# Rounded q and k: stored once per part, and stacked by two loads instead of one

## The chip, the cores and the metric

The kernel runs on one core of one Trainium2 chip. The metric is the device time of one launch in microseconds (us); the kernel before takes 719.64 us (median of 3 runs, 719.59 to 719.88).

The engines are named as in the profile: PE is TensorE (matrix multiplication), PEld its weight loads, DVE is VectorE, ACT is ScalarE, POOL is GpSimd, and SP is the engine whose queue issues nearly all DMAs of this kernel. DMA transfers are done by 16 DMA engines that these queues feed.

## The reference

The reference is one transformer block on 2048 tokens of width 448: layer norm, causal attention with 16 heads of 28 columns in a sliding window of 256 tokens, a residual sum, a second layer norm, a gated feed-forward part of width 1792, and a second residual sum. Cut to what matters:

```python
def _A_ref(x, wqkv, wo):
    H = 16; Dh = D // H; W = 256
    q, k, v = ...                      # x @ wqkv, split by heads
    scores = jnp.einsum("bhqd,bhkd->bhqk", q, k) * (Dh ** -0.5)
    mask = (idx[:, None] - idx[None, :] >= 0) & (idx[:, None] - idx[None, :] < W)
    scores = jnp.where(mask[None, None], scores, -1e9)
    p = _softmax(scores, axis=-1)
    o = jnp.einsum("bhqk,bhkd->bhqd", p, v)
    return o... @ wo

def _B_ref(x, w_gate, w_up, w_down):
    h = _gelu(x @ w_gate) * (x @ w_up)
    return h @ w_down

h = x + _A_ref(_layernorm(x), wqkv, wo)
out = h + _B_ref(_layernorm(h), w_gate, w_up, w_down)
```

All inputs and outputs are float32.

## The kernel before, in words

**Two parts for one number.** The matmuls run in a rounded 32-bit type (`F32R`). To keep float32 precision, a number is split into a rounded high part and the rest, the low part, and a product is made of three: high by high, high by low, low by high. For the scores, the three products are made in a single matmul: the 28 columns of a head are stacked three times along the partitions (84 rows). The stack of q holds high, low, high and the stack of k holds high, high, low, so the sum over the 84 rows is the sum of the three products.

**Projection.** The tokens are cut in 4 chunks (`CS`) of 512. `project_tile(c, m)` makes one of seven output tiles of a chunk with 11 matmuls (line 630): tile m is q or k of one of the groups of 4 heads (112 rows), and 16 further rows that belong to k of the last group. ACT rounds the result from PSUM to the high part, and DVE subtracts to get the low part. The two parts lie in a staging buffer taken by `pk_at`.

**Store.** `put` writes them to a DRAM tile of 112 rows, three rows of 512 per channel (`qk_d`). One DMA (line 640) reads the high part once and writes it to two of the three rows; a second one (line 642) writes the low part. The same pair is issued for the 16 further rows. Each tile thus issues four DMAs.

**Load.** `loads(B)` fetches block B, that is, 4 heads for 512 queries. B counts from 0 to 15, and the group is B % 4, the chunk B // 4. `get` fetches 256 tokens of q or k with one DMA (line 662): 84 partitions (28 channels by three rows) by 4 heads by 256 tokens. q goes to `rq[u]`, k to `rk[u]`, with u = B % 2, so two blocks have buffers. A block loads two halves of 256 tokens, each with one DMA for q and one for k, and from chunk 1 on a further load of the 256 tokens of k from the chunk before.

**Scores and the rest.** `scores` multiplies 128 queries by up to 384 keys of a head (line 680), and DVE takes the maximum over the masked result (line 684). `maxima` turns the maxima into rows that ACT puts beside the q stack (lines 711 and 353). `probs` multiplies again with keys as rows (line 755), now with 104 partitions: the 84 of the stack, zeros, and the rows for the maxima; ACT takes the exponential (line 759). POOL masks the edges (line 774), `attend` multiplies with v (line 793), `drain` normalises, and `output` multiplies with wo (line 851). The second layer norm and the feed-forward part follow (line 1000 and lines after it).

**What sets the order.** Nothing is issued when it is written down. Every step is recorded by `op` with an engine, a cost, a latency, a key and the names that it reads and writes (tokens such as `("rq", u, i)`). `Lists.run` then plays the whole program with these costs: on each engine it takes, among the steps that could start within a short time, the one with the lowest key, and issues it. So the order on every engine comes from the costs, the keys and the dependencies. For a DMA, the planner counts its size, a shared bus, a margin for arrival and at most eight transfers in flight:

```python
if e == "sp" and len(dmas) >= 8:
    t = max(t, dmas[-8])
...
bus = max(bus, t + 1.2) + o.size * 0.0034 + (1.25 if len(dmas) == 2 else 0)
```

Each engine then runs its list in order, and waits on semaphores. The eight DMA semaphores are used in turn, so the ninth DMA waits until the first has landed.

Of the kernel before, what the change touches and what calls it, by code (L numbers as in the profile page):

```python
# [8 lines left out]
F32 = mybir.dt.float32  # L9
# [6 lines left out]
S, D, H, DH, W, F = 2048, 448, 16, 28, 256, 1792  # L16
# [3 lines left out]
GF = 4 * DH  # L20
EPS = 1e-5
SCALE = float(DH) ** -0.5
CS = NT // 4
# [48 lines left out]
def mm(n):  # L72
    return max(n / 2400 + 0.0155, 0.115)
# [156 lines left out]
def block_kernel(ctx: ExitStack, tc, x, wqk_in, wv_in, wo_in, ffn_in, out):  # L230
    nc = tc.nc
# [7 lines left out]
    dram = ctx.enter_context(tc.tile_pool(name="dram", bufs=1, space=bass.MemoryType.DRAM))  # L239

    def f(ap):
        return ap.bitcast(F32)
# [25 lines left out]
    mhl = [mhl_m[:, 128 * i:128 * i + 128] for i in range(2)]  # L268
    rcp = [pool.tile([128, 16], F32, name=f"rcp{i}") for i in range(2)]

    qk_d = [[[dram.tile([GF, 3, 512], F32, name=f"{'qk'[i]}{g}_{c}") for i in range(2)] for c in range(CS)]
            for g in range(NG)]
    ffn_d = dram.tile([128, 1472], F32, name="ffn2")
    xn_d = [dram.tile([D, 128], F32, name=f"xn{t}") for t in range(NT)]
# [20 lines left out]
    rq = [rq_m[:, 2048 * u:2048 * u + 2048].rearrange("p (j t) -> p j t", j=4) for u in range(2)]  # L295
    rk = [rk_m[:, 3072 * u:3072 * u + 3072].rearrange("p (j t) -> p j t", j=4) for u in range(2)]
# [17 lines left out]
    def span(name, lo, n):  # L314
        return (name, lo, lo + n)
# [14 lines left out]
    def WQK(m, h):  # L330
        return ("wqk", m, h)
# [20 lines left out]
    def to_hi(dst, src):  # L352
        nc.scalar.activation(dst, src, AF.Copy)  # L353
# [4 lines left out]
    def dma(key, size, fn, r=(), w=(), cost=0.44, after=()):  # L358
        return op("sp", cost, 0, key, fn, r, w, size=size, after=after)
# [259 lines left out]
    def project_tile(c, m):  # L619
        g, s = divmod(m, 2)  # L620
        cc = 12 * (c % 2)
        hl, both, tok = pk_at()
        B = 4 * c + g
        b = Bank("proj")
        per = 1 if m == 6 else 2
        base = 16 * B - EDGE - (ELAST if c == 3 else 0)
        for a in range(NP):
            h, wb, xb = TERMS[a]
            key = -33 + 6 * m + a / 4 if B < 2 else base - WIN * (1 - (s * NP + a) / (per * NP))
            op("pe", mm(512) + 0.002, 0.403, key, lambda a=a, h=h, wb=wb, xb=xb: nc.tensor.matmul(  # L630
                bank[b.k], wqk[m][:, h, wb, :], xT[:, xb, cc * 128:cc * 128 + 512], start=(a == 0),
                stop=(a == NP - 1)), [span("xT", cc, 4), WQK(m, h)], (), b, tag="proj")
        key = -30 + 6 * m if B < 2 else base
        op("act", 0.49, 0.605, key, lambda: to_hi(hl[0], bank[b.k]), (), [tok[0]], b)
        op("dve", 0.603, 0.698, key, lambda: to_lo(hl[1], bank[b.k], hl[0]), [tok[0]], [tok[1]], b)


        def put(rows, d, name, s, size):
            n = rows.stop - rows.start
            dma(key, 458 * size, lambda: nc.sync.dma_start(  # L640
                d[:, 0:3 - s:2 - s], both[rows, 0:1].to_broadcast([n, 2, 512])), tok[0:1], [(name, 0)])
            dma(key, 229 * size, lambda: nc.sync.dma_start(d[:, 1 + s], both[rows, 1]), tok[1:2], [(name, 1)])
        put(slice(0, GF), qk_d[g][c][s], ("d", g, s, c), s, 1)
        put(slice(GF, 128), qk_d[NG - 1][c][1][16 * m:16 * m + 16], ("d", NG - 1, 1, c, m), 1, 0.15)


    def block(B):
        return B % 4, B // 4
# [3 lines left out]
    def loads(B):  # L652
        g, c = block(B)
        u = B % 2

        def get(s, cc, lo, n, at, key):
            src = qk_d[g][cc][s].rearrange("(j p) b t -> (p b) j t", j=4)[:, :, lo * 128:(lo + n) * 128]
            dst, tok = (rk, "rk") if s else (rq, "rq")
            rd = [(("d", g, 1, cc, m), i) for m in range(WT) for i in range(2)] if s and g == NG - 1 else \
                [(("d", g, s, cc), i) for i in range(2)]  # L660
            rd += [("zk" if s else "zq", u, i) for i in range(2)]
            dma(key, 246 * n, lambda: nc.sync.dma_start(f(dst[u][0:3 * DH, :, at * 128:(at + n) * 128]), src),
                rd, [(tok, u, at + i) for i in range(n)])
        key = 16 * B - (8 if B > 1 else 24)
        if c:
            get(1, c - 1, 2, 2, 0, key)
        for i in range(0, 4, 2):
            get(0, c, i, 2, i, key + 4 * i)
            get(1, c, i, 2, 2 + i, key + 4 * i)
        got[B] = L.ops[-1]  # L670

    def scores(B, i, j):
        g, c = block(B)
        u, m0 = B % 2, i if c else max(i, 2)
        b = Bank("score")
        o = (m0 - i) * 128
        s = 16 * B + 4 * i + j

        def one():
            nc.tensor.matmul(bank[b.k][:, o:384], rq[u][0:3 * DH, j, i * 128:i * 128 + 128],  # L680
                             rk[u][0:3 * DH, j, m0 * 128:(i + 3) * 128], start=True, stop=True)

        def most():
            nc.vector.tensor_tensor_reduce(junk[s % 2][:, o:384], bank[b.k][:, o:384], mask[:, o:384],  # L684
                                           1.0, -BIG, OP.add, OP.max, mx[:, i, j:j + 1])
        op("pe", mm(384 - o), 0.19 + (384 - o) / 2400, s, one,
           [("rq", u, i), *(("rk", u, m) for m in range(m0, i + 3))],
           (), b, tag="score")
        op("dve", 0.08 + (384 - o) * 0.00104, 0.165 + (384 - o) * 0.00106, s, most, ["mask", ("junk", s % 2)],
           [("mx", i, j)], b, tag="most")  # L690
# [53 lines left out]
    def probs(B, m, o):  # L744
        u = B % 2
        lo, hi = parts(m)
        n = (hi - lo + 1) * 128
        G = 512 // n
        for j in range(0, 4, G):
            b = Bank("prob")  # L750
            key = 16 * B + LAG_P + ORDER[m] + j * n / 384

            def some(j=j, b=b):
                for i in range(G):
                    nc.tensor.matmul(bank[b.k][:, n * i:n * i + n], rk[u][0:104, j + i, m * 128:m * 128 + 128],  # L755
                                     rq[u][0:104, j + i, lo * 128:(hi + 1) * 128], start=True, stop=True)

            def exp(j=j, b=b):
                nc.scalar.activation(pp[:, j:j + G, o * 128:o * 128 + n],  # L759
                                     bank[b.k][:, 0:G * n].rearrange("p (g t) -> p g t", g=G), AF.Exp, scale=SCALE)  # L760
            q = [("rk", u, m), *(("pick", u, i) for i in range(4)),
                 *((w, u, i) for i in range(lo, hi + 1) for w in ("rq", "rx"))]
            cost = G * (n / 2400 + 0.009)
            op("pe", cost, cost + 0.17, key, some, q, (), b, tag="prob")
            op("act", 0.065 + G * n * 0.00088, 0.16 + G * n * 0.00088, key, exp, (),
               [p for i in range(G) for p in pp_at(o, hi - lo + 1, j + i)], b, tag="exp")
# [373 lines left out]
    for c in range(CS):  # L1140
# [12 lines left out]
        for g in range(NG):  # L1153
# [9 lines left out]
            at = slots(B)  # L1163
# [117 lines left out]
```

## Time and profile before

| | before |
|---|---|
| median of 3 runs | 719.64 us |
| span of the profiled execution | 718.0 us |
| PE busy | 710.8 us (99%), 5716 instructions |
| DVE, ACT, POOL busy | 396.8, 349.1, 163.4 us |
| granted PE clock | full in all 40 slices |
| DMA queue of SP | 80.98 MB, 39.5% of 16 engines' span |
| loads of q and k stacks (line 662) | 76 of 336 KB |

The profiled execution spans 718.0 us; the median of the runs is 1.6 us above it. The slices of the page cover 18 us each. The attention part takes the slices up to about 325 us; in them the DMA engines are 0.6 to 0.9 busy up to 288 us. From about 327 us on, PE works on the feed-forward part (line 1000) almost alone. In rows of groups, the name left of the arrow is what is written, the name right of it what is read; "SPq" is the issue of a DMA on SP's queue, with the time that the issue itself took. In the wait lists the numbers are the sum in us, how many times, and the longest.

### The profile page before, as it was taken

The numbers are of one execution on the slowest core, as the hardware profiler recorded it, in microseconds if no ns is written. First come the engines' busy times: TensorE is split into PE (matmuls) and PEld (weight loads), VectorE is DVE, ScalarE is ACT, GpSimd is POOL, SyncE is SP. The second block draws the span as 40 slices with busy tenths as digits, with TensorE's granted clock in tenths as the row PEclk, the third lists the DMA queues.
The fourth block names the chain that finished last, engine by engine and source line by source line (L and its number), as shares of the span: only waits on it lengthen the run. The fifth ranks groups of instructions, "written<-read, shape, count | busy, mean of one in ns | idle before, by whom it ended". The sixth has DMA issues, their size and how long they took to land.

```text
span 718.0 us, 14862 instructions
## 1 busy us (share of the span) xinstructions
PE 710.8 (99%) x5716; PEld 592.1 (82%) x5716; DVE 396.8 (55%) x1034; ACT 349.1 (49%) x787; POOL 163.4 (23%) x284
## 2 busy tenths in 40 slices
PE   8999999999999999999999999999999999999997
PEld 7887778788878887778888888888888888888886
DVE  7957688988788789857544312335132235132224
ACT  7738676768667679875533222244222223222221
POOL 5604553644454466541000000000000000000000
PEclk9999999999999999999999999999999999999999
DMA  8895976787858787223641000021000000001002
GB/s 312 265 309 177 279 190 178 198 255 204 221 131 239 202 255 180 64 77 73 188 136 43 1 2 1 1 84 55 33 1 2 1 1 1 2 1 52 22 32 103
DMA packets 96926, 82.03 MB, mean 114 GB/s; under 512 B 41736, under 2 KB 83016, under 8 KB 96840
## 3 DMA queue, kind: packets, MB, share of 16 engines
q1 hardware_dynamic: 96712, 80.98, 39.5%
q8 instruction: 45, 0.74, 0.4%
q14 instruction: 25, 0.20, 0.1%
q10 hardware_dynamic: 144, 0.11, 0.0%
HBM read 50.27 MB, written 31.03 MB: 113 GB/s over the span
## 4 chain that ended last, share of the span: by engine, by line
PE 94%; ACT 2%; DVE 2%; POOL 1%; issue 1%; DMA 0%; DVEq 0%; ACTq 0%
PE bank L1000 52%; PE bank L630 10%; PE bank L755 7%; PE bank L680 6%; PE bank L793 6%; PE bank L578 5%; PE bank L851 4%; PE bank L1024 3%; PE bank L408 1%; ACT rq L353 1%; ACT xn L403 0%; DMA hres<-in_x_dram 0%; DVE hres L854 0%; DVE hres L1102 0%; PE bank L711 0%
## 5 line engine op out<-in xcount | busy, mean ns | idle before, releaser
L684 DVE CUSTOM_DVE_ANT_0 mt<-bank,mt 128x384 bf16<-128x384 f32 (+2 forms) x256 | 127.5, 527 | 33.9 <-PE bank L680 31.0
L1066 DVE TENSOR_TENSOR mt<-bank,mt 128x512 f32<-128x512 f32 x54 | 37.1, 688 | 142.2 <-ACT mt L1064 142.2
L759 ACT ACTIVATE pp<-bank 128x384 f32<-128x384 f32 (+1 forms) x212 | 103.2, 533 | 22.5 <-PE bank L755 18.3
L630 PE MATMUL bank<-xT 128*128 128x512 f32 x308 | 94.6, 397 | 0.0
L774 POOL TENSOR_SCALAR_AFFINE_SELECT pp<-pp 128x512 f32<-128x512 f32 x120 | 75.0, 640 | 67.0 <-ACT pp L759 62.7
L1064 ACT ACTIVATE mt<-bank 128x512 f32<-128x512 f32 x54 | 32.2, 596 | 117.1 <-PE bank L1000 117.1
L1000 PE MATMUL bank<-xT,rk 64*128 64x512 f32 x656 | 82.0, 388 | 0.0
L1000 PE MATMUL bank<-xT,rec 64*128 64x512 f32 x656 | 82.0, 388 | 0.0
L755 PE MATMUL bank<-rq,rk 104*128 104x384 f32 (+2 forms) x352 | 81.4, 305 | 0.4 <-ACT pp L759 0.3
L680 PE MATMUL bank<-rk,rq 84*128 84x384 f32 (+2 forms) x256 | 80.6, 340 | 0.0
L1102 DVE TENSOR_TENSOR hres<-bank,hres 128x448 f32<-128x448 f32 (+1 forms) x65 | 35.7, 611 | 67.8 <-PE bank L1000 66.0
L1000 PEld LDWEIGHTS bank<-xT,rec 64*128 64x128 f32 x656 | 63.0, 184 | 12.2
L1000 PEld LDWEIGHTS bank<-xT,rk 64*128 64x128 f32 x656 | 63.0, 184 | 12.2
L755 PEld LDWEIGHTS bank<-rq,rk 104*128 104x128 f32 x352 | 59.1, 189 | 13.7 <-ACT pp L759 3.8
L1000 PE MATMUL bank<-xT,proj 64*128 64x512 f32 x533 | 66.9, 389 | 0.4 <-ACT e L1006 0.3
L1006 ACT ACTIVATE e<-bank 1x1 f32<-1x1 f32 x162 | 25.7, 159 | 79.4 <-PE bank L1000 78.8
L630 PEld LDWEIGHTS bank<-xT 128*128 128x128 f32 x308 | 55.6, 189 | 6.2 <-ACT xT L353 0.2
L1000 PEld LDWEIGHTS bank<-xT,proj 64*128 64x128 f32 x533 | 51.0, 184 | 11.0 <-ACT e L1006 1.1
L680 PEld LDWEIGHTS bank<-rk,rq 84*128 84x128 f32 x256 | 46.8, 189 | 11.7 <-DVE mx L684 1.7
L353 ACT ACTIVATE rq<-bank 8x512 fp32r<-8x512 f32 x64 | 37.7, 589 | 27.9 <-PE bank L711 26.9
L578 PE MATMUL bank<-proj,xT 128*128 128x448 f32 (+1 forms) x220 | 47.5, 334 | 0.0
L793 PE MATMUL bank<-pp,v 128*29 128x384 f32 (+2 forms) x704 | 45.4, 388 | 0.0
(147 smaller groups left out, 1075.1 us busy)
## 6 DMA issues: line engine op xcount, KB each, us to landing
rk<-k SPq DMA_DIRECT2D x44, 336.0 KB
rq<-q SPq DMA_DIRECT2D x32, 336.0 KB
v<-in_ffn_dram SPq DMA_DIRECT2D x7, 736.0 KB
q<-proj SPq DMA_DIRECT2D x11, 448.0 KB
raw<-in_ffn_dram SPq DMA_DIRECT2D x6, 736.0 KB
xn<-xn SPq DMA_DIRECT2D x72, 56.0 KB
xT<-xn SPq DMA_DIRECT2D x20, 192.0 KB
hres<-in_x_dram SPq DMA_DIRECT2D x16, 224.0 KB
```

Source lines behind the costliest of these rows:

```text
L353: nc.scalar.activation(dst, src, AF.Copy)
L578: op("pe", mm(224 * n), 0.29 if n == 1 else 0.38, key + a / 16, lambda a=a, h=h, wb=wb, xb=xb: nc.tensor.matmul(bank[b.k][:, 0:224 * n], x ...
L630: op("pe", mm(512) + 0.002, 0.403, key, lambda a=a, h=h, wb=wb, xb=xb: nc.tensor.matmul(bank[b.k], wqk[m][:, h, wb, :], xT[:, xb, cc * 128 ...
L680: nc.tensor.matmul(bank[b.k][:, o:384], rq[u][0:3 * DH, j, i * 128:i * 128 + 128], rk[u][0:3 * DH, j, m0 * 128:(i + 3) * 128], start=True, ...
L684: nc.vector.tensor_tensor_reduce(junk[s % 2][:, o:384], bank[b.k][:, o:384], mask[:, o:384], 1.0, -BIG, OP.add, OP.max, mx[:, i, j:j + 1])
L755: nc.tensor.matmul(bank[b.k][:, n * i:n * i + n], rk[u][0:104, j + i, m * 128:m * 128 + 128], rq[u][0:104, j + i, lo * 128:(hi + 1) * 128] ...
L759: nc.scalar.activation(pp[:, j:j + G, o * 128:o * 128 + n], bank[b.k][:, 0:G * n].rearrange("p (g t) -> p g t", g=G), AF.Exp, scale=SCALE)
L774: nc.gpsimd.affine_select(a, a, pattern=[[0, 4], [-cm, 128]], compare_op=op_, fill=0.0, base=0, channel_multiplier=cm)
L793: nc.tensor.matmul(bank[b.k][32 * j:32 * j + DH + 1, lo * 128:(hi + 1) * 128], v[:, at_v(4 * c - 2 + m), 4 * g + j, :], pp[:, j, at[m] * 1 ...
L1000: nc.tensor.matmul(bank[bk.k][:, 0:n], w, m, start=bool(start), stop=bool(stop), tile_position=(64 * x, 0), skip_group_check=True)
L1066: op("dve", 0.605, 0.702, key + 2 * NP, lambda: nc.vector.tensor_tensor(blocks(g2), src(1), blocks(g2), op=OP.mult), [*G2, *held[1]], G2, ...
L1102: nc.vector.tensor_tensor(hres[:, t, c0:c0 + w], bank[b.k][:, c0:c0 + w], hres[:, t, c0:c0 + w], op=OP.add),
```

## The change

The DRAM tile has two rows per channel instead of three, and each part is stored once. In q's tile the order is high, low; in k's tile it is low, high. A stack is made by two DMAs: one puts the high part in rows 56 to 83 (28 partitions), the other both parts in rows 0 to 55 (56 partitions, channel by channel). The product of high by high now comes from the last 28 rows, and the other two products from the first 56. The first of the two loads depends on the store of the high part alone, the second on both. Their sizes, as the planner counts them, are 82 and 164 per 128 tokens instead of 246, and the store of the high part counts 229 instead of 458. The steps that read the stacks now name two tokens per buffer and range (0 and 2). The sum that a score is made of has the same terms; the PE instructions have the same shapes.

```diff
-    qk_d = [[[dram.tile([GF, 3, 512], F32, name=f"{'qk'[i]}{g}_{c}") for i in range(2)] for c in range(CS)]
+    qk_d = [[[dram.tile([GF, 2, 512], F32, name=f"{'qk'[i]}{g}_{c}") for i in range(2)] for c in range(CS)]
...
         def put(rows, d, name, s, size):
-            n = rows.stop - rows.start
-            dma(key, 458 * size, lambda: nc.sync.dma_start(
-                d[:, 0:3 - s:2 - s], both[rows, 0:1].to_broadcast([n, 2, 512])), tok[0:1], [(name, 0)])
-            dma(key, 229 * size, lambda: nc.sync.dma_start(d[:, 1 + s], both[rows, 1]), tok[1:2], [(name, 1)])
+            for i in range(2):
+                dma(key, 229 * size, lambda i=i: nc.sync.dma_start(d[:, i ^ s], both[rows, i]), tok[i:i + 1], [(name, i)])
...
         def get(s, cc, lo, n, at, key):
-            src = qk_d[g][cc][s].rearrange("(j p) b t -> (p b) j t", j=4)[:, :, lo * 128:(lo + n) * 128]
+            d = qk_d[g][cc][s][:, :, lo * 128:(lo + n) * 128]
             dst, tok = (rk, "rk") if s else (rq, "rq")
...
-            dma(key, 246 * n, lambda: nc.sync.dma_start(f(dst[u][0:3 * DH, :, at * 128:(at + n) * 128]), src),
-                rd, [(tok, u, at + i) for i in range(n)])
+            at_ = slice(at * 128, (at + n) * 128)
+            dma(key, 82 * n, lambda: nc.sync.dma_start(
+                f(dst[u][2 * DH:3 * DH, :, at_]), d[:, s].rearrange("(j p) t -> p j t", j=4)),
+                [r for r in rd if type(r[0]) is str or not r[1]], [((tok, 2), u, at + i) for i in range(n)])
+            dma(key, 164 * n, lambda: nc.sync.dma_start(
+                f(dst[u][0:2 * DH, :, at_]), d.rearrange("(j p) b t -> (p b) j t", j=4)),
+                rd, [((tok, 0), u, at + i) for i in range(n)])
...
-           [("rq", u, i), *(("rk", u, m) for m in range(m0, i + 3))],
+           [*((("rq", x), u, i) for x in (0, 2)), *((("rk", x), u, m) for m in range(m0, i + 3) for x in (0, 2))],
...
-            q = [("rk", u, m), *(("pick", u, i) for i in range(4)),
-                 *((w, u, i) for i in range(lo, hi + 1) for w in ("rq", "rx"))]
+            q = [(("rk", 0), u, m), (("rk", 2), u, m), *(("pick", u, i) for i in range(4)),
+                 *((w, u, i) for i in range(lo, hi + 1) for w in (("rq", 0), ("rq", 2), "rx"))]
```

## The prediction

> **What bounds the kernel now.** I read the profile page first (busy shares, slices, chain), then busy time by windows, then what TensorE waited for, then the issue rows of the stores and loads, and last the order in which the built program of each version puts its instructions.
>
> ```profile
> span 718.0 us, 14862 instructions
> PE 710.8 (99%) x5716; PEld 592.1 (82%) x5716; DVE 396.8 (55%) x1034; ACT 349.1 (49%) x787; POOL 163.4 (23%) x284
> DMA  8895976787858787223641000021000000001002
> PE 94%; ACT 2%; DVE 2%; POOL 1%; issue 1%; DMA 0%; DVEq 0%; ACTq 0%
> 20.00:60.00 40.00, 39.73 (x230) 34.64 (x229) 31.32 (x101) 22.44 (x45) 12.45 (x26) 1.00 0.90 277
> 260.00:300.00 40.00, 39.97 (x293) 31.25 (x292) 37.27 (x119) 33.07 (x73) 29.75 (x46) 1.00 0.63 159
> sum 307.00, PE 306.45 PEld 246.55 DVE 245.07 ACT 218.77 POOL 147.85; mean PE 38.31 PEld 30.82 DVE 30.63 ACT 27.35 POOL 18.48
> PE bank L1223 <- POOL ident L504: 2.1, 1, 2.1
> PE bank L1000 <- ACT e L1006: 0.3, 1, 0.3
> PE bank L755 <- ACT pp L759: 0.3, 1, 0.3
> PE bank L408 <- ACT xn L403: 0.2, 1, 0.2
> PE bank L1000 <- DVE hres L854: 0.2, 1, 0.2
> PEld bank L755 <- ACT pp L759: 3.8, 14, 0.5
> PEld bank L755 <- ACT rq L353: 1.8, 8, 0.3
> PEld bank L680 <- DVE mx L684: 1.7, 4, 0.6
> ```
>
> TensorE is busy for 710.8 of 718.0 us and the chain is 94% PE with 0% DMA. The summed windows from 20 to 327 us (the stage where the changed code works) hold 306.45 us of PE in 307. The granted clock there is 1.00. DMA engines are 0.90 busy from 20 to 60 us, yet the list of PE's waits names no DMA: none of the stacks that the score matmuls (L680) read came late. So the fixed amount of matmul work sets the time. A faster store cannot shorten it; a load that lands after its reader is due lengthens it one for one, because PE runs in order and the feed-forward stage behind it is packed too.
>
> **The change part by part.**
>
> Stores. In the first two rows here the high part goes out as 448 KB (the same rows twice) and the low part as 224 KB.
>
> ```profile
> q<-proj SPq DMA_DIRECT2D x11, 448.0 KB
> q<-proj SPq DMA_DIRECT2D x11, 224.0 KB
> rk<-k SPq DMA_DIRECT2D x44, 336.0 KB
> rq<-q SPq DMA_DIRECT2D x32, 336.0 KB
> L662 SPq DMA_DIRECT2D rk<-k x44: 308/442/996, 30.9 to 282.4; - x44
> L662 SPq DMA_DIRECT2D rq<-q x32: 308/354/1396, 26.1 to 281.9; - x32
> ```
>
> Each of 28 projected tiles stores 224 KB less (and 32 KB less for the 16 rows that belong to the last group): 28 x 256 KB, about 7.2 MB off the queue before 265 us. Nothing on PE waited for these bytes, so I book 0. Both ends: at best the load behind a store lands 224 KB sooner, which is worth time only if it was late (it was not); at worst nothing.
>
> Loads. The 76 loads of 336 KB become 76 of 112 KB plus 76 of 224 KB: the same bytes, 76 more issues on SP. With the medians above, a half block (one rq, one rk) takes 0.35 + 0.44 us of issue now and twice that after; so its last load is issued about 0.8 us later behind the event that frees it. What lies behind these loads on SP are the second half's loads, the stores of the next tile and the transposes of the layer norm (L447, L455): all shift by up to 4 more issues per block, 1.6 us. The second halves keep 2 to 4 us more cover than the first halves, so I price only first halves.
>
> The planner. It sees different sizes and dependencies and hence writes another order, not only two issues for one. In the built order the matmuls up to the first score matmul of block 0 stand as before; then that matmul comes 5.7 us of PE work earlier. PE has the same 5364 matmul instructions in both. I counted, for the first half of each block, the PE work between the last matmul that its loads must wait for (through SP's order) and the first matmul that reads them, at the spacing of these two rows (16 matmuls of 512 columns start 0.23 us apart, 24 of 448 start 0.20 us apart):
>
> ```profile
> 317.85 3.92 PE L1024 MATMUL bank<-xT,rq 128*128 128x512 f32 x16
> 321.60 5.03 PE L851 MATMUL bank<-proj,ohl 128*128 128x448 f32 x24
> ```
>
> This cover, before and after, in us for blocks 2 to 15: 8.7/6.0, 7.6/5.5, 6.7/5.1, 7.8/6.9, 5.6/6.0, 6.8/7.5, 7.0/7.2, 8.9/5.6, 10.5/7.0, 5.5/9.1, 7.8/7.0, 6.0/5.7, 7.9/5.6, 5.8/8.8. It falls in ten blocks of fourteen; the least goes from 5.5 to 5.1.
>
> How much is needed? The trace gives intervals from the last issue of a first half to its first reader that were enough. Blocks 2, 4, 9 and 13, issue and reader:
>
> ```profile
> 64.50 0.43 SPq L662 DMA_DIRECT2D rk<-k  x1
> 71.94 0.34 PE L680 MATMUL bank<-rk,rq 84*128 84x128 f32 x2
> 92.59 0.44 SPq L662 DMA_DIRECT2D rk<-k  x1
> 100.55 0.51 PE L680 MATMUL bank<-rk,rq 84*128 84x384 f32 x2
> 177.67 0.78 SPq L662 DMA_DIRECT2D rk<-k  x1
> 187.09 0.52 PE L680 MATMUL bank<-rk,rq 84*128 84x384 f32 x2
> 247.12 0.43 SPq L662 DMA_DIRECT2D rk<-k  x1
> 252.78 0.39 PE L680 MATMUL bank<-rk,rq 84*128 84x384 f32 x1
> ```
>
> The intervals are 7.44, 7.96, 9.42 and 5.66 us; block 13's 5.66 is the shortest that the trace shows to suffice. After the change each becomes the old one, less the lost cover, less 0.8: block 2 7.44 - 2.7 - 0.8 = 3.9; block 4 7.96 - 1.6 - 0.8 = 5.6; block 9 9.42 - 3.3 - 0.8 = 5.3; block 13 5.66 - 0.3 - 0.8 = 4.6. The others stay above 5.66. Short of 5.66 by 1.7, 0.1, 0.3 and 1.1: together 3.2 us is the upper end. The lower end is 0, since 5.66 may hold reserve and the last load now carries 224 KB instead of 336. Nothing says which end is nearer; I take the middle, +1.6 us. Block 0 loses 2.8 us of cover too, but its loads have the second copies of four stores, about 1 MB, less ahead of them in the fullest stage; I book 0, with 2 us as its other end.
>
> More waits. A score matmul now reads two loads for q and two for k; the built program has 91 separate wait instructions on PE instead of 60.
>
> ```profile
> L680 PEldq EVENT_SEMAPHORE  x35: 51/51/600, 37.4 to 291.0; - x35
> 40.66 0.34 PE L680 MATMUL bank<-rk,rq 84*128 84x128 f32 x2
> ```
>
> A wait takes 51 ns in PE's own queue. The first of them stands at 37.4, the matmul that needs it at 40.66: the queue runs ahead, so queued matmuls cover it. I book 0; without the cover it is 31 x 0.051 = 1.6 us.
>
> Other engines. The same DVE and ACT work in another order. It can remove the 1.8 us in which L755's weight loads waited for ACT (rows above) or make similar waits elsewhere; ends -1.8 and +1.8, taken as 0, since the numbers of instructions are equal.
>
> Sum: 0 + 1.6 + 0 + 0 = +1.6 us. The profiled execution spans 718.0; the median of the runs, 719.64, stands 1.6 above that span. 718.0 + 1.6 (around the span) + 1.6 = 721.2 us.
>
> A rule against this change stands in the Trainium skill, page "DMA: Bandwidth & Descriptors", section "Rules for kernel authors": two transfers to separate partition ranges run on the same engines and gain nothing over one, and small transfers are to be joined. The same page's "Anatomy of one DMA" puts a fixed 2.0 us on each; if each split load paid that in series on the path, 15 blocks would lose some 30 us (an estimate from the page). This trace speaks against the series, as the next rows show.
>
> ```profile
> 0.79 2.55 DMA hres<-in_x_dram
> 63.05 1.40 SPq L662 DMA_DIRECT2D rq<-q  x1
> 65.02 0.39 SPq L662 DMA_DIRECT2D rq<-q  x1
> 65.46 0.44 SPq L662 DMA_DIRECT2D rk<-k  x1
> ```
>
> A load of 224 KB alone lands 2.55 us after its issue, but four loads of block 2 are issued within 2.9 us (63.05 to 65.90, with the row at 64.50 above), each long before the one ahead could land.
>
> **The rivals.**
>
> *Hidden.* All loads still land in time; the built order keeps at least 5.1 us of cover and 5.66 held reserve. Time 719.6, within 0.5.
>
> *Faster.* Block 0 starts 5.7 us of PE work earlier, with more projection matmuls left to fill the stage where L755 waited for ACT's maxima (1.8 us in 8 waits). If these go and no load is late: 719.6 - 1.8 = 717.8. It decides if the PEld waits on ACT rq vanish. Against it: another order finds other small waits, and PE's idle in 20 to 327 us is only 0.55 us in all.
>
> *Late everywhere.* Loads, stores and transposes share one SP queue whose issues stretch when DMA is full (L662 up to 1396 ns). If 76 more issues make each of 15 first halves late by 0.4 us: 719.6 + 6 = 725.6. For it: 0.90 DMA share from 20 to 60 us. Against: 7.2 MB less, and no DMA among PE's waits now.
>
> *In series.* Each first half pays a whole load more, 15 x 2.55 = 38 us: 757.9. The issue rows speak against it.
>
> **How the numbers follow.** Some loads late by 0 to 3.2 us in all: 0.54, giving 721.2 with its own range 719.6 to 722.9. Hidden 0.11, faster 0.23, late everywhere 0.10, in series 0.02. A change under 0.2% (1.44 us) is about what a measurement of this kernel can't tell from none; the line to "slower" is 721.1. Spread evenly over 0 to 3.2, a little over half of the first case lies above it: slower 0.30 + 0.10 + 0.02 = 0.42, same 0.24 + 0.11 = 0.35, faster 0.23. The range 717.6 to 724.6 leaves out the upper part of the last two cases and the far side of "faster".
>
> **What would show it.** Right: PE's busy time stays near 710.8 and the span grows by idle before L680's group, with DMA rq<-q or rk<-k as the releaser in blocks 2, 9 or 13; the DMA share falls by some tenth before 265 us; the wait rows on PE's queue rise by 31. Wrong: no DMA among PE's waits and a span under 719 (hidden or faster), or late loads in every block. An order that leaves PE idle before L755 or L793 would also break the sum, since I price those at nothing.

## The result, and the profile after

The changed kernel takes 722.59 us (median of 7 runs, 721.45 to 723.52) against 719.88 us for the kernel before beside it (719.59 to 720.33): a ratio of 1.0039, 95% interval 1.0028 to 1.0049. It is slower, by some 2.7 us. Two profiles of it exist: one from these runs (that execution took 723.2 us, its span is 721.5 us) and one from a later set of runs, called "changed again" below (721.82 us, span 720.1 us). Ratios here leave disturbed executions out, so they need not be the exact quotient of the two medians.

The page of the changed kernel, then what PE waited for (sum in us, times, longest), busy time by windows (window, length, PE, PEld, DVE, ACT, POOL, granted clock, DMA share, GB/s), the issue rows of the loads, and the waits in PE's own queue of instructions:

```profile
span 721.5 us, 14977 instructions
PE 711.8 (99%) x5716; PEld 592.4 (82%) x5716; DVE 397.2 (55%) x1034; ACT 352.3 (49%) x787; POOL 162.9 (23%) x284
...
q1 hardware_dynamic: 94192, 73.64, 36.4%
...
PE bank L683 <- DMA rk<-k: 1.2, 1, 1.2
...
PEld bank L758 <- ACT rq L353: 2.2, 7, 0.6
...
20.00:330.00 310.00, 307.69 (x2103) 246.53 (x2101) 245.98 (x777) 222.37 (x445) 147.76 (x243) 1.00 0.65 173
330.00:721.50 391.50, 386.38 (x3513) 330.31 (x3513) 135.87 (x227) 113.58 (x318) 3.21 (x8) 1.00 0.12 38
...
rk<-k SPq DMA_DIRECT2D x44, 224.0 KB
...
rk<-k SPq DMA_DIRECT2D x44, 112.0 KB
...
L683 PEldq EVENT_SEMAPHORE  x68: 51/51/519, 32.3 to 293.3; - x68
```

The same two windows of the kernel before, and of the second profile of the changed kernel:

```profile
20.00:330.00 310.00, 309.29 (x2125) 248.81 (x2125) 248.01 (x782) 219.60 (x447) 148.04 (x244) 1.00 0.72 198
330.00:718.00 388.00, 383.93 (x3493) 327.84 (x3491) 133.57 (x221) 113.15 (x316) 3.02 (x8) 1.00 0.12 38
```

```profile
20.00:330.00 310.00, 308.70 (x2117) 248.13 (x2118) 247.65 (x780) 222.78 (x446) 147.96 (x243) 1.00 0.66 175
330.00:720.10 390.10, 385.03 (x3503) 329.46 (x3501) 134.56 (x223) 113.30 (x316) 3.21 (x8) 1.00 0.12 38
```

PE's work is what it was (711.8 us busy against 710.8), SP's queue moves 73.64 MB in place of 80.98, and each load of 336 KB has become one of 112 and one of 224 KB. The windows divide the loss. From 330 us on, the work is the feed-forward part, packed on PE. The busy time in that window therefore tells how much PE work was still to be done at 330 us, and the idle time in it (length less busy) tells what is lost at the end.

- Work left at 330 us: 383.93 before, 386.38 after, so the attention part is 2.45 us late. In the second profile it is 385.03, 1.10 us late.
- Idle after 330 us: 388.00 - 383.93 = 4.07 before, 391.50 - 386.38 = 5.12 after, 5.07 in the second profile. The end of the kernel costs 1.0 us more in both.

2.45 + 1.05 is the 3.5 us between the spans; 1.10 + 1.00 is the 2.1 us of the second profile. Of the 2.45 us, 1.24 is one wait of PE for a load of k, in block 6; the second profile has no such wait, so it comes in some executions only. The rest, about 1.1 to 1.2 us, both profiles share. So there are three pieces: 1.0 us at the end, 1.1 us spread over the attention part, and in some executions a late load of 1.2 us.

Two rows show where a part of the 1.1 us lies, the first of the second profile of the changed kernel, then the projection's matmuls there and in the kernel before:

```profile
260.00:300.00 40.00, 39.51 (x288) 30.36 (x287) 34.55 (x110) 34.13 (x71) 28.81 (x45) 1.00 0.61 155
```

```profile
L630 PE MATMUL bank<-xT 128*128 128x512 f32 x308 | 96.3, 400 | 0.1
```

```profile
L630 PE MATMUL bank<-xT 128*128 128x512 f32 x308 | 94.6, 397 | 0.0
```

Between 260 and 300 us PE is idle for 0.49 us (0.47 in the first profile), against 0.03 before. The same 308 projection matmuls are busy for 1.7 us more; with the order of before they stay at 94.6, and with the order of the change they are at 96.4 even when the old DMAs are used (the two kernels of the next section). Matmuls overlap on PE (these last 0.4 us each and start some 0.23 us apart), so such a busy time is not a share of the 1.1 us that could be added to others.

### The profile page after: what moved, and what is told of

The parts are those of the page before. It is cut to its first block, busy times and chain, and to the rows that moved or that the text cites. A ratio compares the mean times of both kernels' runs of the same rounds, so it can differ in the third digit from the quotient of the medians.

```text
span 721.5 us, 14977 instructions
## 1 busy us (share of the span) xinstructions
PE 711.8 (99%) x5716; PEld 592.4 (82%) x5716; DVE 397.2 (55%) x1034; ACT 352.3 (49%) x787; POOL 162.9 (23%) x284
## 3 DMA queue, kind: packets, MB, share of 16 engines
q1 hardware_dynamic: 94192, 73.64, 36.4%
## 4 chain that ended last, share of the span: by engine, by line
PE 88%; ACT 3%; DVE 2%; DMA 2%; POOL 1%; issue 1%; SPq 1%; DVEq 0%; POOLq 0%; ACTq 0%
PE bank L1003 51%; PE bank L630 8%; PE bank L758 6%; PE bank L683 6%; PE bank L796 5%; PE bank L578 4%; PE bank L854 4%; PE bank L1027 2%; DMA rk<-k 1%; ACT rk L353 1%; ACT xn L403 1%; POOL bnve L377 1%; DMA rq<-q 1%; ACT rq L353 1%; PE bank L408 0%
## 5 line engine op out<-in xcount | busy, mean ns | idle before, releaser
L762 ACT ACTIVATE pp<-bank 128x384 f32<-128x384 f32 (+1 forms) x212 | 105.4, 535 | 35.6 <-PE bank L758 22.7
L630 PE MATMUL bank<-xT 128*128 128x512 f32 x308 | 96.3, 399 | 0.1
L758 PE MATMUL bank<-rq,rk 104*128 104x384 f32 (+2 forms) x352 | 82.3, 305 | 0.4 <-ACT rq L353 0.3
L758 PEld LDWEIGHTS bank<-rq,rk 104*128 104x128 f32 x352 | 59.2, 189 | 14.0 <-ACT pp L762 2.7
L578 PE MATMUL bank<-proj,xT 128*128 128x448 f32 (+1 forms) x220 | 49.3, 334 | 0.0
```

The lines of the kernel that those rows point to most:

```text
L578: op("pe", mm(224 * n), 0.29 if n == 1 else 0.38, key + a / 16, lambda a=a, h=h, wb=wb, xb=xb: nc.tensor.matmul(bank[b.k][:, 0:224 * n], x ...
L762: nc.scalar.activation(pp[:, j:j + G, o * 128:o * 128 + n], bank[b.k][:, 0:G * n].rearrange("p (g t) -> p g t", g=G), AF.Exp, scale=SCALE)
```

## Content or order: two kernels that take one each

The change alters two things: what the DMAs move, and, through sizes and dependencies, the order that the planner writes. Theory A: the split loads are the cost (late first halves, the step of the prediction). Theory B: the order is the cost.

**Order of before, DMAs of the change.**

```diff
 # the changed kernel, with the planner's view of before
-            for i in range(2):
-                dma(key, 229 * size, lambda i=i: ...)
+            dma(key, 458 * size, lambda: nc.sync.dma_start(d[:, s], both[rows, 0]), tok[0:1], [(name, 0)])
+            dma(key, 229 * size, lambda: nc.sync.dma_start(d[:, 1 - s], both[rows, 1]), tok[1:2], [(name, 1)])
...
+            def both_loads():
+                nc.sync.dma_start(f(dst[u][2 * DH:3 * DH, :, at_]), d[:, s].rearrange("(j p) t -> p j t", j=4))
+                nc.sync.dma_start(f(dst[u][0:2 * DH, :, at_]), d.rearrange("(j p) b t -> (p b) j t", j=4))
+            dma(key, 246 * n, both_loads, rd, [(tok, u, at + i) for i in range(n)])
```

> The order of the kernel before on every engine, with the DMAs of the change: each part stored once, and two loads issued one after the other where one stood (the planner still counts one load of the old size). Theory A (the split loads land late by themselves): the cover of block 6 and its like is that of before, but each first half's last load is issued about 0.8 us later; PE waits on DMA appear and the time is 720.5 to 722. Theory B (the other order makes the loss, the split costs nothing where the cover is that of before): within 0.5 us of the kernel before, about 719.9, and no DMA among PE's waits, since the smallest cover stays 5.5 us.

Measured: 719.81 us (719.66 to 720.3), ratio 0.9997, interval 0.9988 to 1.0006. Busy time by windows:

```profile
20.00:330.00 310.00, 309.29 (x2125) 249.24 (x2125) 248.02 (x782) 219.55 (x447) 148.15 (x244) 1.00 0.67 175
330.00:717.90 387.90, 383.95 (x3493) 329.03 (x3490) 133.60 (x221) 113.10 (x316) 3.01 (x8) 1.00 0.12 38
```

PE is busy for the same 309.29 us as before, and the work left at 330 us is the same within 0.02 us. The DMA share falls from 0.72 to 0.67. PE's own queue has 66 separate waits on the score line (35 before), as many as in the changed kernel to within two. So 7.3 MB less to store, 76 more issues and these waits are together worth nothing here, either way.

**Order of the change, DMAs of before.** The first load step issues nothing, and the second one loads all 84 rows.

```diff
+            dma(key, 229 * size, lambda: nc.sync.dma_start(
+                d[:, 0:3 - s:2 - s], both[rows, 0:1].to_broadcast([n, 2, 512])), tok[0:1], [(name, 0)])
...
-            dma(key, 82 * n, lambda: nc.sync.dma_start(...),
+            dma(key, 82 * n, lambda: None,
...
-                f(dst[u][0:2 * DH, :, at_]), d.rearrange("(j p) b t -> (p b) j t", j=4)),
+                f(dst[u][0:3 * DH, :, at_]), d.rearrange("(j p) b t -> (p b) j t", j=4)),
```

> The order of the changed kernel on every engine, with the DMAs of the kernel before: the high part stored twice, one load of 84 partitions issued where the second of the two stood, nothing where the first stood. Theory A (late split loads): the one load per buffer lands sooner after the event that frees it, the wait of 1.2 us before block 6's scores goes, and the time is about 720.5. Theory B (the order): block 6 still has SP's long issue behind four transposes and the wait for it stays, the time is 721.5 to 722.5.

Measured: 723.85 us (723.33 to 724.96), ratio 1.0056 (1.0042 to 1.007). What PE waited for, and the window to the end:

```profile
PE bank L855 <- DVE hres L858: 0.7, 1, 0.7
PE bank L684 <- DMA xT<-xn: 0.6, 1, 0.6
PE bank L684 <- DMA rk<-k: 0.4, 1, 0.4
...
330.00:722.10 392.10, 386.75 (x3517) 330.24 (x3514) 136.40 (x227) 113.70 (x319) 3.21 (x8) 1.00 0.13 38
```

The loss is all there without any of the change's DMAs, and by the medians it is 1.3 to 1.8 us larger than with them. That is more than either theory had forecast, and the wait at block 6, which theory B had expected to stay, is not in this profile; two other waits behind DMAs are. The four corners settle the main question: order of before 719.9 and 719.8, order of the change 723.85 with the old DMAs and 722.1 to 722.6 with the new ones. Theory A falls; the order is the cost. Within that order the lighter DMAs seem to help: the ranges touch (723.33 to 724.96 here, 721.45 to 723.79 over the twelve executions of the changed kernel in its two sets of runs), and whether the stores or the loads do it is not separated.

**The changed kernel once more**, as the base for comparisons on one chip:

> The changed kernel as it is, beside the others: 722.6 us, between 721.5 and 723.5, with a wait of about 1.2 us for rk before one score group of block 6. If the wait moves to another block or changes by over 1 us between executions, its spread (2.1 us over seven runs, against 0.7 before) comes from late loads.

Measured: 722.07 us (721.82 to 723.79), ratio 1.0036 (1.0023 to 1.0049). The expected wait for rk is not there: no DMA is among PE's waits.

## The late load of block 6

In the first profile the issues of SP ahead of block 6, and the reader:

```profile
113.47 1.87 SPq L447 DMA_DIRECT2D xn<-xn  x4
115.44 1.99 SPq L661 DMA_DIRECT2D rq<-q  x1
117.79 0.31 SPq L664 DMA_DIRECT2D rq<-q  x1
118.15 0.41 SPq L661 DMA_DIRECT2D rk<-k  x1
118.61 0.49 SPq L664 DMA_DIRECT2D rk<-k  x1
...
123.60 0.59 PE L683 MATMUL bank<-rk,rq 84*128 84x384 f32 x2 [1.24 <-DMA rk<-k]
```

The same four loads in the second profile, where nothing waited:

```profile
115.71 0.41 SPq L661 DMA_DIRECT2D rq<-q  x1
116.48 1.00 SPq L664 DMA_DIRECT2D rq<-q  x1
117.54 0.45 SPq L661 DMA_DIRECT2D rk<-k  x1
118.04 0.39 SPq L664 DMA_DIRECT2D rk<-k  x1
...
122.45 0.52 PE L683 MATMUL bank<-rk,rq 84*128 84x384 f32 x2
```

The new order puts four transposes of the layer norm (L447) right ahead of block 6's loads. In the execution with the wait, the first load behind them takes 1.99 us to issue in place of 0.41, and the four issues span 115.44 to 119.10, 3.66 us. The last load of k lands 4.85 us after its issue began, and PE's wait ends with it. In the second profile the four issues span 2.72 us, the last load lands after 3.95 us, and its reader starts 4.41 us after the issue without a wait. Two kernels of a later section that keep this order ahead of block 6 agree: where the first issue took 2.08 us PE waited 1.5 us, and where it took 0.41 us nothing waited. So in these four profiles the long first issue and the wait come together or not at all; what makes the issue long in some executions is not known.

I moved the four transposes behind the eight loads, and left the rest of the order as it was:

```diff
+            if kind == "ln1" and t == 15:
+                late.append(o)
...
+    for o, fn in L.emit:
+        if o in late:
+            moved.append(fn)
+            continue
+        out.append(fn)
+        if o is got[6]:
+            out += moved
```

> The changed kernel with one thing moved: the four layer-norm transposes of token tile 15 (line 447), which stand on SP's queue just ahead of block 6's loads, are issued after these eight loads; every other engine's order is that of the changed kernel. Theory A1 (the wait at block 6 comes from the transposes: behind them the first load takes 1.99 us to issue): the wait of 1.2 us goes and the time falls by about 1.2 us, to 721.4. Theory A2 (four issues instead of two are too many for block 6's cover of 6.0 us wherever the transposes are): a wait of 0.5 us or more stays and the time falls by less than 0.7 us.

Measured: 722.22 us (721.43 to 723.33), ratio 1.0032 (1.0019 to 1.0044). The wait at block 6 is not in its profile, but another one is, after 280 us:

```profile
PE bank L685 <- DMA rk<-k: 0.8, 1, 0.8
...
330.00:720.40 390.40, 385.44 (x3507) 330.18 (x3503) 134.88 (x225) 113.43 (x317) 3.21 (x8) 1.00 0.12 38
```

So moving what stood before the load does not bring the time down: this order has more than one load without reserve. Since the wait is absent in one plain execution too, this run does not show that the transposes caused it; that stays open.

## Is it this order, or any other order?

Theory P: the order of before is a favourable one among those that this planner writes, and any new plan gives it up. Theory Q: what the change tells the planner makes the order worse. Four kernels re-plan by other means.

```diff
 # before, other margin
-MARGIN = 0.7
+MARGIN = 0.75
 # before, small store: only the planner's number
-            dma(key, 458 * size, lambda: nc.sync.dma_start(
+            dma(key, 229 * size, lambda: nc.sync.dma_start(
 # after, large store: only the planner's number
-                dma(key, 229 * size, lambda i=i: ...
+                dma(key, (458, 229)[i] * size, lambda i=i: ...
 # after, long margin
-MARGIN = 0.7
+MARGIN = 1.4
```

> The kernel before with one planning constant altered: the lead that the planner keeps behind each transfer is 0.75 us in place of 0.7. Every DMA is the one of before, only the written-out order differs. Theory P (the order of before is a favourable one among those that this planner can draw, and any new plan gives it up): 720.5 to 724, ratio 1.001 to 1.006, with the idle time of PE in the blocks' maxima and probabilities and not behind a DMA. Theory Q (the order that the change draws is worse because of what the change tells the planner: smaller stores, eight loads a stage): within 0.2% of before, 719.2 to 720.6.

Measured: 720.93 us (720.59 to 722.95), ratio 1.0020 (1.0012 to 1.0029). Not one DMA differs from before; 0.05 us more of margin costs about 1 us.

> The kernel before, its DMAs unaltered, but the planner is told 229 in place of 458 KB for the store of the high part. Only the order differs. This is the stores' half of what the change tells the planner. P: 720.5 to 724. Q with the stores as the cause: 721.5 to 722.6, as the changed kernel; Q with the split loads as the cause: 719.2 to 720.6.

Measured: 726.2 us (724.4 to 728.61), ratio 1.0088 (1.0074 to 1.0101): the worst of all, again with the DMAs of before.

> The changed kernel with its DMAs, but the planner is told 458 KB for the store of the high part as before. This is the loads' half of what the change tells the planner. P: 720.5 to 724, and not the same number as the changed kernel. Q with the split loads as the cause: 721.5 to 722.6; Q with the stores as the cause: 719.2 to 720.6.

Measured: 721.36 us (721.27 to 722.04), ratio 1.0022 (1.0013 to 1.0031).

> The changed kernel with the planner's lead behind each transfer at 1.4 us in place of 0.7, so that every reader is placed 0.7 us later behind its load. If late loads are the cost (the step of the prediction), the wait of PE for a load is gone and the time falls to 719.6 to 720.6. P: no DMA among PE's waits, and still 720.5 to 724, since the idle time behind ACT's and DVE's results stays.

Measured: 721.11 us (719.66 to 721.79), ratio 1.0010 (1.0002 to 1.0019); the profiled execution, of 719.67 us, has a span of 717.9 us, the one of before.

P holds in its direction: none of the five other plans that ran (these four and the change's own) is faster than before. Four lie from 0.2% to 0.9% above it; the long margin lies 0.1% above, and in a second set of runs (next section) it can't be told from before. Q can't be told from it by so few: the store's size alone re-planned to the worst, the loads' split alone to 721.36, both together to 722.6. For the long margin itself P had forecast 720.5 or more; its median is there, its best executions are not. That a longer margin takes the changed kernel's best executions to the time of before shows that its DMAs don't stand in the way of a good order.

## How a small hole becomes a large one

In the kernel before with the small store, one wait of PE is 2.3 us long. Its wait row, and busy time by windows around it (the eighth entry is the granted clock):

```profile
PE bank L711 <- DVE mhl L704: 2.3, 1, 2.3
...
286.00:288.00 2.00, 0.28 (x2) 0.00 (x0) 1.90 (x2) 0.65 (x3) 2.00 (x3) 1.00 1.04 254
288.00:290.00 2.00, 1.40 (x4) 1.00 (x4) 1.56 (x6) 0.90 (x2) 2.00 (x3) 0.61 0.79 160
290.00:292.00 2.00, 2.00 (x17) 0.78 (x20) 1.02 (x6) 1.94 (x4) 0.99 (x1) 0.50 0.69 119
...
296.00:298.00 2.00, 2.00 (x7) 1.71 (x7) 0.80 (x4) 0.75 (x2) 1.02 (x4) 0.50 0.00 0
298.00:300.00 2.00, 2.00 (x10) 1.58 (x8) 1.19 (x5) 1.98 (x5) 0.28 (x1) 0.83 0.00 0
```

After the hole the granted clock is 0.50 in each stretch from 290 to 298 us, and below 1.00 in the two beside them. The work lost is 2 x (0.39 + 4 x 0.50 + 0.17) = 5.1 us, so what follows the hole of 2.3 us costs twice as much as the hole. The clock is not all that makes this order slow: the profiled execution, 728.61 us at a mean granted clock of 0.992, is the slowest of six, and the fastest, 724.40 us, had 1.0.

The times of the changed kernel with the long margin lie in two groups, 719.66 to 720.40 us with a granted clock of 1.0, and 721.11 to 721.79 with 0.997 or 0.998. It ran a second time, to catch an execution from the upper group:

> The changed kernel with the lead of 1.4 us once more, for a second profile. Its executions lay in two heaps, 719.7 to 720.4 with a granted clock of 1.0 and 721.1 to 721.8 with 0.997 to 0.998. If the upper heap is a hole of PE that the throttle answers, a profile from it shows a hole of 1 us or more at 280 to 300 us and a granted clock under 0.9 in the slices behind it, as in the profile of the kernel before with the small store; if it is not, the clock is lower elsewhere without a hole. Median again 719.7 to 721.5.

Measured: 720.24 us (719.55 to 721.54), ratio 1.0007 (0.9998 to 1.0015); the profiled execution took 721.54. The hole is not where the expectation had it but at 62 us. The first profile of this kernel, then the second:

```profile
62.00:64.00 2.00, 1.49 (x7) 1.11 (x7) 0.99 (x5) 2.00 (x6) 2.00 (x3) 1.00 0.42 81
64.00:66.00 2.00, 2.00 (x11) 1.66 (x11) 1.93 (x10) 2.00 (x7) 2.00 (x4) 1.00 0.85 251
66.00:68.00 2.00, 2.00 (x16) 1.83 (x14) 1.96 (x9) 2.00 (x5) 1.85 (x4) 1.00 0.74 208
```

```profile
PE bank L758 <- ACT pp L762: 0.7, 1, 0.7
...
62.00:64.00 2.00, 1.38 (x7) 1.10 (x7) 0.88 (x5) 1.98 (x6) 1.93 (x3) 1.00 0.40 89
64.00:66.00 2.00, 2.00 (x9) 1.63 (x9) 1.93 (x10) 2.00 (x6) 2.00 (x3) 0.77 0.72 215
66.00:68.00 2.00, 2.00 (x7) 1.70 (x6) 1.47 (x7) 1.45 (x3) 1.52 (x4) 0.50 0.61 192
68.00:70.00 2.00, 2.00 (x15) 1.86 (x14) 1.13 (x5) 1.26 (x3) 1.67 (x6) 0.88 0.81 227
...
330.00:719.80 389.80, 386.15 (x3519) 330.51 (x3519) 136.25 (x227) 113.28 (x318) 3.21 (x8) 1.00 0.12 38
```

The same wait of 0.7 us stands in both. Once the clock answers with 0.77, 0.50 and 0.88 in three stretches of 2 us, which is 2 x (0.23 + 0.50 + 0.12) = 1.7 us of work lost; once it doesn't. That is most of the 1.9 us between the two spans. Over both sets of runs the thirteen executions from 719.55 to 720.61 us show a granted clock of 0.999 or 1.0, the nine from 721.04 to 721.79 us one of 0.997 or 0.998. The Trainium skill, page "TensorE: Matmul & The Clock Gate", section "What's actually happening", has the clock fall to one half after an idle window of about 3.4 us. The one half agrees with the 0.50 here; the length does not: the half clock followed 2.3 us of idle and, in one of two executions, 0.7 us, and the measurement decides. That the hole is what the clock answers is read from the order of events; what else must come together for the fall is not shown.

In the two profiles of the changed kernel itself the granted clock is 1.00 in every stretch of 2 us from 8 to 330 us, so this is not where its own 2.1 to 3.5 us went.

## The microsecond at the end

In the changed kernel the last store is issued at 717.55 us and the span ends at 721.5, 3.9 us later; before, 715.03 and 718.0, 3.0 us. (The expectations below count from the end of that issue, which takes 0.33 us.) The waits of SP in the last 8 us, and the queue of instruction packets in the last 4 us (packets, MB, share), after:

```profile
SPq L1280 <- DMA out_dram<-hres: 2.4, 3, 1.4
...
q14 instruction: 1, 0.01, 0.5%
```

Before, no instruction packet lies in the last 4 us, and SP's wait row is:

```profile
SPq L1277 <- DMA out_dram<-hres: 1.6, 1, 1.6
```

Each store lands in 16 parts. In the trace of the changed kernel an instruction packet of 8 KB starts at 717.92 us, and for each of the last three stores 15 parts land together and one comes 0.9 to 1.0 us later (for the last one: 719.51 us, and 720.53). Before, all 16 parts of the last store land between 716.81 and 716.98. Theory F: DVE fetches its program in pieces, and a longer program (1220 rows of DVE in the trace, 1209 before; the 1034 that work are the same, the eleven more are waits) puts a fetch among the last stores. The test adds memsets of one element to DVE's program, inside the feed-forward part:

```diff
+    spare = [pool.tile([1, 1], F32, name=f"spare{i}") for i in range(2)]
...
-        op("dve", 0.6, 0.7, key + 2 * NP, lambda: to_lo(gh(1), blocks(g2), gh(0)), [*G2, at[0]], [at[1]], port=True)
+        op("dve", 0.6, 0.7, key + 2 * NP, lambda: (to_lo(gh(1), blocks(g2), gh(0)),
+                                                 nc.vector.memset(spare[n % 2], 0.0) if 10 <= n < 21 else None),
+           [*G2, at[0]], [at[1]], port=True)
```

> The kernel before with eleven more instructions on DVE, each a memset of one element of a tile that nobody reads, one behind each of eleven of the feed-forward part's rests of gh (L1066), so that DVE's program is as long as the one of the changed kernel (1220 rows in the trace, 1209 before). The orders are otherwise those of before. Theory F (the microsecond between the last output issue and the end of the span, 3.6 us in the changed kernel and 2.6 before, is a fetch of instructions by DVE that meets the last stores on one DMA engine, and it depends on the length of DVE's program): 720.7 to 721.1, the span near 719.0, an instruction packet in the last 5 us, and one of the 16 landings of the last store a microsecond behind the others. Rival: the memsets themselves cost nothing beside PE and the fetch has another cause: 719.7 to 720.2 with the tail of before.

Measured: 722.33 us (722.12 to 722.91), ratio 1.0033 (1.0021 to 1.0046). SP's waits in the last 8 us, and the window to the end:

```profile
SPq L1280 <- DMA out_dram<-hres: 2.5, 1, 2.5
...
330.00:721.10 391.10, 385.99 (x3499) 373.06 (x3495) 134.04 (x234) 113.31 (x316) 3.21 (x8) 1.00 0.12 37
```

The end is there: a fetch at 717.45, one part of the last store a microsecond behind the rest, idle after 330 us 391.10 - 385.99 = 5.11. Made from the kernel before by eleven instructions that compute nothing, it is what F forecast. But the time is 1.2 us above F's range of 720.7 to 721.1: PE's busy time in this window grew by 2.06 us and PEld's by 45. The feed-forward part itself is 1.6 us slower: the last 3300 matmuls of the trace take 364.3 us from the first start to the last, 362.7 before. The rest was already late at 330 us. The next run repeats it.

**The changed kernel with sixteen such memsets** (`10 <= n < 26`), so that the fetch comes earlier:

> The changed kernel with sixteen more such memsets on DVE, so that the fetch falls some sixteen of DVE's instructions earlier, ahead of the last stores. Theory F: about 1.0 us less than the changed kernel, 721.0 to 721.7, and 2.6 us between the last output issue and the end. Rival: 722.0 to 722.7 as the changed kernel, with 3.6 us there.

Measured: 722.67 us (722.24 to 723.69), ratio 1.0040 (1.0027 to 1.0053). The fetch is at 714.34, and from the issue of the last store to the end it is 2.9 us, close to the 3.0 of the kernel before. The feed-forward part is slower by the same amount (364.5 us for the last 3300 matmuls, 362.9 in the second profile of the changed kernel), with PEld at 373.25 from 330 us on. The two tiles `spare` of one element each stand ahead of other tiles in the kernel, which so come to lie at other addresses. So the third kernel writes an element of `mx` instead, and moves no tile:

```diff
+                                                 nc.vector.memset(mx[0:1, 0, 0:1], 0.0) if 10 <= n < 26 else None),
```

> The changed kernel with sixteen more memsets on DVE in the feed-forward part, this time on one element of mx, which is no longer read there, so that no tile moves by a byte. In the two kernels before this one the tile of one element that was added took all later tiles to other addresses, and the feed-forward part grew by 1.6 us with PEld's busy time between 330 and 700 us at 358 us against 316. Theory F (end: the fetch of instructions) with theory L (the 1.6 us are the tiles' addresses): PEld at 316 us there, 2.6 us between the last output issue and the end, and 721.0 to 721.7, 1.0 us less than the changed kernel. F without L (the memsets slow the weight loads): 2.6 us at the end, 722.2 to 723.7 and PEld at 358. Neither: 722.0 to 722.7 and 3.6 us at the end.

Measured: 722.01 us (720.69 to 724.29), ratio 1.0030 (1.0021 to 1.0039).

```profile
PE bank L683 <- DMA rk<-k: 1.5, 1, 1.5
...
SPq L1282 <- DMA out_dram<-hres: 1.5, 4, 0.6
...
330.00:721.10 391.10, 386.93 (x3519) 330.02 (x3515) 136.48 (x244) 113.87 (x319) 3.22 (x8) 1.00 0.12 38
```

PEld is at 330.02 and the last 3300 matmuls take 362.9 us, so it was not the memsets that made the feed-forward part slower but where the tiles lie. Each weight load lasts 184 to 185 ns in the mean in all these kernels; what grew is the time in which one or another of them runs. Why the tiles' place does this is not shown. Idle after 330 us is 391.10 - 386.93 = 4.17, the end of before, so F holds in the profile. It holds over all traces too: in the five with 1220 rows of DVE one part of each of the last three stores comes late, in the nine others, with 1200 to 1215 or with 1236 rows, none does. Why a packet that takes 0.31 us holds a part back by a microsecond stays open. F with L had put the median at 721.0 to 721.7, and it is no better than "changed again" (722.01 against 722.07): this profile has the wait for block 6's load again, 1.5 us of it, and the eleven executions spread over 3.6 us. How often the late load comes is not settled by these runs, so the saved microsecond is shown in the profile and not in the median.

## Why the prediction was right, and where not

The direction and the size came out: 721.2 with a range of 717.6 to 724.6 against 722.59, and slower as the likeliest sign. The step that was to carry it did not, so the number is right by luck: +1.6 was priced as late loads in four blocks that never waited, and what came was 1.1 us in the attention part, 1.0 us at the end and, in some executions, a late load in another block.

- That PE bounds, and a late load lengthens the time one for one: right. The spans differ by what PE's work was late at 330 us and by the end; PE has the same 5716 instructions.
- Stores, booked 0: right with the order of before (719.81). In the new order the lighter DMAs, stores and loads together, are worth 1.3 to 1.8 us by the medians, which the sum did not have: it had no row for a content that helps only in a worse order.
- Loads, short in blocks 2, 4, 9 and 13, +1.6: wrong mechanism. None of these blocks waits in either profile. One wait comes in block 6, whose cover I had rising from 5.6 to 6.0. Two steps failed. The first is "its last load is issued about 0.8 us later". It took the medians of issue times and left out what the new order puts ahead on SP: four transposes, a first issue of 1.99 us, and 3.66 us for the four issues. With the old order, twice the issues cost no wait at all. (The list of covers falls in nine blocks of fourteen, not ten; the sum doesn't use the count.)
- The second is "Short of 5.66", the measure of lateness: too strict. In block 6 of the second profile 4.41 us were enough, and the load landed in 3.95 us (4.85 in the first). Blocks 4 and 9, for which 5.6 and 5.3 us were forecast, have 5.2 us in both profiles and do not wait. The reserve that the lower end of 0 allowed for was there.
- More waits, booked 0: right on PE. The wait row of PE's queue on this line goes from 35 to 68 instructions of 51 ns, and with the order of before they cost nothing. On DVE the new order brought eleven more waits, and these moved a fetch into the end of the kernel.
- Other engines, booked 0 with ends of 1.8 either way: this is the term that was mis-sized. The order as a whole is worth 1.1 us in the attention part in both profiles, within these ends. Only part of it shows as waits (idle from 20 to 330 us is 0.71 before and 1.30 in "changed again"); the rest lies inside PE's busy time, in the projection's matmuls above all, and can't be added up row by row.
- The end of the span, which I carried over unchanged, holds 1.0 us that no view of the kernel before could show.
- The Trainium skill's rule on two transfers to separate partition ranges (page "DMA: Bandwidth & Descriptors", section "Rules for kernel authors"): with the order held, the split neither gained nor lost (0.9997), so the runs agree that it gains nothing. The 2.0 us of "Anatomy of one DMA" on the same page were not seen in series; that section gives them for DMAs issued by GpSimd, and these loads are issued on SP.
- Rivals: "hidden" is what happens with the order of before; "faster" did not come, the weight loads of L758 still wait for ACT, 2.2 us in 7 waits (2.0 in the second profile) against 1.8 in 8; "late everywhere" and "in series" are excluded by the same run.

## What to carry to other kernels

Where a planner writes the order, an edit to a transfer is two edits: measure it once with the old order held fixed and once with the new order and the old transfers, before any of it is credited to the transfer. A tuned order on a packed engine is one draw among many: here none of five other plans was faster, four lost 0.2% to 0.9%, one of these by 0.05 us more of margin. Ask of each stage not only how much cover a load has but what the new order has put ahead of it on its queue.

## What the runs showed of the hardware

- A hole of 0.7 us on PE was followed in one execution by a granted clock of 0.50 and 1.7 us of lost work, and in another by none; a hole of 2.3 us was followed by 8 us and more at 0.50, 5.1 us of lost work.
- With a fetch of 8 KB of instructions among the last stores, one of 16 parts of each of the last three came 0.9 to 1.0 us late, so eleven instructions without work made the kernel's end 1.0 us longer. The Trainium skill, page "Runtime: NRT & Kernel Launch", section "Instruction fetch mechanics", calls the cost of such a refill mostly hidden. Here it shows, in the stores that end the kernel.
- Two tiles of one element, which moved other tiles, took PEld's busy time after 330 us from 327.84 to 373.06 us and made the last 3300 matmuls 1.6 us longer (364.3 us against 362.7), while a single weight load kept its 184 ns.
